# Gated mix of two attentions: where path A's denominators are inverted, and where its late products stand

## The chip, the core and the metric

The kernel runs on one NeuronCore of a Trainium2 chip. The metric is the time of one execution on the device in microseconds; lower is better. The time before is the median of three runs, 987.2 us (984.97 to 989.04).

## What is computed

The input x has 2048 tokens of width 448, in 16 heads of 28. Path A is a linear attention with a learned feature map, path B an ordinary softmax attention, and a gate for each token mixes the two:

```
phi(u) = concat(softmax(u @ w_phi), softmax(-(u @ w_phi)))     per head
kv  = phi(k)^T v;   z = sum over tokens of phi(k)
a   = ((phi(q) kv) / (phi(q) z + 1e-6)) @ woA
b   = softmax(q k^T / sqrt(28)) v @ woB
out = g * a + (1 - g) * b,     g = sigmoid(sum(x * gate_w))
```

The division in path A is by one number per head and token, the **denominator**. All of it is in float32; products that need the precision are split into a high and a low part and run as two or three matmuls.

## The kernel before

The order of the work on PE, DVE, ACT and POOL is the order in which the code is written; only SP's queue of transfers is ordered by a scheduler, from the order of the code and its own estimate of readiness. SP issues its transfers one after another, and each waits in the queue until what it reads is there; what stands behind it waits with it.

The program has three stretches. Up to about 196 us path A's keys, path B's projections and the gate are made. From there to about 332 us runs the stretch that the change is in: path A's queries, numerators, denominators and output, with the first of path B's value projections at its end. From about 364 us on path B's scores and values run (a third of PE's time each), to the end.

The loop of the second stretch counts i; q = i - 16, **y = q - 1**, and tb = y // 2. A path A **block** is 256 tokens, eight blocks (0 to 7) in all; two iterations handle one block. In the order of the code an iteration with q up to 15 projects a tile of queries (`pq`), copies it (`pcq`, ACT), takes its extremes over each head (`extq`, two DVE reductions, L423 and L424), forms the exponents on POOL (L429, L431), and exponentiates them on ACT (L434).

From q = 8 on each iteration has a **unit of maxima** (`mx_unit`, L260 to L265): four small matmuls into four PSUM banks (two `pmd`, two `pmb`), two Relu on ACT (`rl<-pmd`), and two DVE instructions that add and reduce (`rl<-pmb,rl`). These maxima are path B's row maxima. The four banks are the only ones for that use, so a unit's matmuls on PE wait until DVE has read the unit before. Iterations with q from 19 to 25 have a second unit at their end.

The chain of one block b, with the iterations before the change:

- **numerators** (`numer`, L529), at the end of y = 2b + 4: matmuls into two banks `pn`, which ACT copies to `oUa` (L381). Four rows of each bank are the denominators; SP gathers them with two transfers `dena<-oUa` (L384) of 8 KB, spread over 128 partitions.
- **inverses** (`normalize2`), in y = 2b + 5: DVE's RECIPROCAL on `dena` (L389, 128x32), two transfers `rda<-dena` to DRAM (L393), and one transfer `rsa<-rda` (L394) that reads them back repeated over 32 partitions each, 512 KB: the **broadcast**.
- **product** (`normalize3`), in y = 2b + 8: DVE multiplies `oUa` by `rsa` (L400, 128x1024).
- **split** (`normalize4`), in y = 2b + 9: ACT casts `oTa` (L408), POOL subtracts for the low part (L409).
- **output** (`out_a`), in y = 2b + 10 and 2b + 11: twelve matmuls `poa` (L109), which ACT scales by the gate to `ga` (L544); SP stores `gad<-ga` (L545).

`oUa` has three buffers, `dena`, `rda` and `rsa` two each. Iterations with q from 18 on also project a tile of path B's values (`pvb`, eleven matmuls), and transpose features (`pft`, copied by ACT at L519) as long as there are any. SP's queue also carries loads for the maxima (`qp`, `kp`, `kt`, L176).

The part of the loop body that sets the order before the change:

```
if q in (0, 1) or q >= 8:
    mx_unit()
if y >= 9 and y % 2 and tb - 4 < 8:
    oTs[tb - 4] = normalize4(ta, num.pop(tb - 4), f"a{tb - 4}", 2)
...
if y >= 8 and y % 2 == 0 and tb - 4 < 8:
    num[tb - 4] = normalize3(*num[tb - 4], 2)
if y >= 5 and y % 2 and tb - 2 < 8:
    num[tb - 2] = normalize2(ta, *num[tb - 2], f"a{tb - 2}", 2)
```

Of the kernel before, what the change touches and what calls it, by code (L numbers as in the profile page):

```python
# [24 lines left out]
NT = S // P  # L25
# [16 lines left out]
def gated_mix_kernel(ctx, tc, xT, wqkB, wvB, wvA, wkAT, wqAT, phi, woA, woB,  # L42
# [26 lines left out]
    def ps_mx(nm):  # L69
        return ps.tile([P, 512], F32, tag="mx", name=nm, bufs=psn[1])  # L70
# [113 lines left out]
    def mx_load(g, c):  # L184
        mxs[("kc", g, c)] = mx_rows(mx_tile("kc", f"kc{g}_{c}", 5), range(4), k_d[g], range(4),
                                    c * 512)

    def mx_query(gq):
        g, qb = divmod(gq, NQ)
        mxs[("qc", gq)] = mx_rows(mx_tile("qc", f"qc{gq}", 3), range(4), q_d[g], range(4), qb * 512)  # L190

    def pair_load(g, c):

        hp, b = divmod(c, 2)
        heads = (2 * hp, 2 * hp + 1)
        r = mx_tile("kc", f"kp{g}_{c}", 5)
        t = mx_tile("kd", f"kt{g}_{c}", 1)
        mx_rows(r, (0, 1), k_d[g], heads, b * 1024)
        mx_rows(r, (2, 3), k_d[g], heads, b * 1024 + 512)
        mx_rows(t, (2, 3), k_d[g], heads, b * 1024)  # L200
        mxs[("kp", g, c)] = r

        def sub():
            for i in (2, 3):
                js = slice(32 * i, 32 * i + DH)
                nc.gpsimd.tensor_sub(r[js], f32(r[js]), f32(t[js]))

        subs.append(sub)

    def pair_query(gq, hp):  # L210
        g, qb = divmod(gq, NQ)
        mxs[("qp", gq, hp)] = mx_rows(mx_tile("qc", f"qp{gq}_{hp}", 3), range(4), q_d[g],
                                      (2 * hp, 2 * hp + 1) * 2, qb * 512)

    def mx_fin():
        while mxs["fin"]:
            mxs["fin"].pop(0)()
# [5 lines left out]
    def mx_reduce(gq):  # L223

        col = 64 * gq
        n = 2 if gq < GM else 4
        r = 4 * (gq % 8)

        def reduce():
            nc.vector.tensor_reduce(  # L230
                red.rearrange("p (t c) -> p t c", t=4)[:, :, r:r + 4],
                part[:, col:col + 16 * n].rearrange("p (k t h) -> p t h k", t=4, h=4),
                AX.X, ALU.max)
            nm_of[gq] = True

        mxs["fin"].append(reduce)

    def mx_unit():

        u = mxs["u"]  # L240
        if u == NF:
            return
        mx_fin()
        mxs["u"] = u + 1
        gq, r = divmod(u, 16)
        g, qb = divmod(gq, NQ)
        c, qt = divmod(r, 4)
        hp, b = divmod(c, 2)
        col = 64 * gq + 16 * b + 4 * qt + 2 * hp
        if r in (4, 9) and gq + 1 < GM:  # L250
            pair_query(gq + 1, r // 9)
        if r == 4 and gq + 1 == GM:
            mx_query(GM)
        qc, kc = mxs[("qp", gq, hp)], mxs[("kp", g, c)]

        pm = [ps_mx(f"pm{'ddbb'[j]}{u}_{j % 2}") for j in range(4)]
        for j in range(4):
            i = (j + 2) % 4
            js = slice(32 * i, 32 * i + DH)
            nc.tensor.matmul(pm[j], qc[js, qt * P:(qt + 1) * P], kc[js, :], start=True, stop=True,  # L260
                             tile_position=(32 * i, 0))
        for i in range(2):
            rl = rlp.tile([P, 512], F32, tag="rl", name=f"rl{u}_{i}", bufs=psn[2])
            nc.scalar.activation(rl, pm[i], AF.Relu)  # L264
            nc.vector.tensor_tensor_reduce(rl, pm[2 + i], rl, 1.0, LOWEST, ALU.add, ALU.max,  # L265
                                           part[:, col + i:col + i + 1])
        if gq + 1 < GM and qt == 3 and qb == NQ - 1:
            pair_load(g + 1, c)
        if gq + 1 == GM and qt == 3:
            mx_load(GM // NQ, c)  # L270
        if r == 15:
            mx_reduce(gq)
# [114 lines left out]
    def normalize2(pool, oU, den, nm, n):  # L387

        nc.vector.reciprocal(den, den)  # L389
        rd = dr.tile([4, n * 512], F32, tag=f"rd{n}", name=f"rd{nm}", bufs=2)  # L390
        rs = pool.tile([P, n, 512], F32, tag="rs", name=f"rs{nm}", bufs=n)
        for k in range(n):
            nc.sync.dma_start(rd[:, k * 512:(k + 1) * 512], den[:, k, :])  # L393
        nc.sync.dma_start(rs.rearrange("p n q -> p (n q)"),  # L394
                          rd.unsqueeze(1).to_broadcast([4, 32, n * 512]))
        return oU, rs

    def normalize3(oU, rs, n):

        (nc.gpsimd if n == 1 else nc.vector).tensor_mul(oU, oU, rs)  # L400
        return oU

    def normalize4(pool, oU, nm, n):

        oTn = []
        for k in range(n):
            oT = pool.tile([P, 2, 512], F32R, tag="oT", name=f"oT{nm}_{k}", bufs=3 * n - 2)
            (nc.scalar.copy if n == 2 else nc.gpsimd.tensor_copy)(oT[:, 0, :], oU[:, k, :])  # L408
            nc.gpsimd.tensor_sub(oT[:, 1, :], oU[:, k, :], f32(oT[:, 0, :]))  # L409
            oTn.append(oT)  # L410
        return oTn
# [48 lines left out]
    fk, va, fq, fT_of, num, oTs = {}, {}, {}, {}, {}, {}  # L460
# [242 lines left out]
    for i in range(2 * NT + 11):  # L703
        t, q = i, i - NT
        y = q - 1
        tb = y // 2
# [11 lines left out]
        if q == 2:  # L718
            bk_s.close()
            ta_s = ExitStack()  # L720
            ta = ta_s.enter_context(tc.tile_pool(name="ta", bufs=1, reuse_waits="tile"))
# [24 lines left out]
            fk[t - 1] = features2(fk[t - 1], f"k{t - 1}")  # L746
        if q in (0, 1) or q >= 8:
            mx_unit()
        if y >= 9 and y % 2 and tb - 4 < 8:
            oTs[tb - 4] = normalize4(ta, num.pop(tb - 4), f"a{tb - 4}", 2)  # L750
        if q > 0:
# [5 lines left out]
        take_subs()  # L757
        if t == 1:
            pair_load(0, 3)
        if y >= 8 and y % 2 == 0 and tb - 4 < 8:  # L760
            num[tb - 4] = normalize3(*num[tb - 4], 2)
        if y >= 5 and y % 2 and tb - 2 < 8:
            num[tb - 2] = normalize2(ta, *num[tb - 2], f"a{tb - 2}", 2)
        if t < NT:
            value_a(t)
            if t % 2 and t < NT - 4:
# [29 lines left out]
            turn(y - 2)  # L796
        if NT + 3 <= q < NT + 10:
            mx_unit()
        if q == NT + 6:
            ps_s_.close()  # L800
            ps = ps_s_.enter_context(tc.tile_pool(name="psv", bufs=1, space=PSUM, reuse_waits="tile"))
            psn[:2] = 2, 6
# [439 lines left out]
```

## Time and profile before

| | |
|---|---|
| median of three runs | 987.2 us (984.97 to 989.04) |
| the profiled execution's own time | 986.38 us |
| its span, first to last instruction | 984.6 us |
| mean granted TensorE clock | 0.998 |
| PE busy in 196 to 332 us | 131.23 of 136 us |
| DVE busy in 196 to 332 us | 89.08 of 136 us |

The profile is of one execution. The engines are PE (TensorE's matmuls), PEld (its weight loads), DVE (VectorE), ACT (ScalarE), POOL (GpSimd) and SP (SyncE, which issues the transfers; SPq in the rows). A row of a timeline has the start in us from the beginning of the span, the duration in us, the engine, the line of the kernel, the operation, what it writes and reads, the shape, and the number of instructions merged; idle time of the engine before it and what ended that stand in brackets. A row of the chain of waits has start, duration and the piece of work. A row of the stretches has the stretch, its length, busy time of an engine with its number of instructions, the granted clock, the share of the transfer engines in use, and GB/s.

### The profile page before, as it was taken

What the parts mean: (1) busy time and instruction counts of PE and PEld (TensorE: products, weight loads), DVE (VectorE), ACT (ScalarE), POOL (GpSimd) and SP (SyncE); (2) the same over time, 40 slices, a digit from 0 to 9 for tenths busy, and PEclk for the clock granted to TensorE, in tenths of its full rate; (3) what the DMA queues carried; (4) which work ended last, traced back from release to release, by engine and by line L of the source; (5) the groups of instructions that cost most, each with busy time, mean ns of one, the idle gap of its engine ahead of it and who ended that gap; (6) DMA issues with size and microseconds to landing.
All of it is one profiled execution on the core that took longest, in us unless ns stands there. A gap on an engine that the chain in (4) does not pass through costs nothing.

```text
span 984.6 us, 22550 instructions
## 1 busy us (share of the span) xinstructions
PE 973.6 (99%) x8510; PEld 602.9 (61%) x8510; DVE 716.0 (73%) x1338; ACT 752.2 (76%) x1442; POOL 228.1 (23%) x236
## 2 busy tenths in 40 slices
PE   9999999999999999999999999999999999999998
PEld 8777877787767765555555555545555555555555
DVE  5566767888735678888888888888888888885112
ACT  4455655577855688988988888888898898887662
POOL 1135435586732810031011011011011011010010
PEclk9999999999999999999999999999999999999999
DMA  8873110112223234121132121122231222100441
GB/s 295 315 255 114 37 53 32 44 51 73 96 91 100 85 120 130 38 62 41 62 93 69 39 63 41 60 82 66 69 83 41 64 63 65 41 21 30 142 150 57
DMA packets 56140, 84.49 MB, mean 86 GB/s; under 512 B 17216, under 2 KB 23984, under 8 KB 56032
## 3 DMA queue, kind: packets, MB, share of 16 engines
q1 hardware_dynamic: 56032, 83.06, 27.2%
q8 instruction: 67, 1.10, 0.5%
q14 instruction: 41, 0.34, 0.1%
HBM read 54.86 MB, written 27.78 MB: 84 GB/s over the span
## 4 chain that ended last, share of the span: by engine, by line
PE 89%; DMA 6%; DVE 2%; ACT 1%; issue 1%; SPq 0%; DVEq 0%; ACTq 0%
PE g L861 29%; PE pv L1006 26%; PE pk L127 4%; PE pva L127 4%; PE pqk L109 3%; PE g L288 3%; PE pq L109 3%; PE poa L109 3%; PE pob L109 3%; PE pmd L260 3%; DMA dena<-oUa 2%; PE pvb L127 2%; DMA qkd<-ev 2%; PE pvb L109 1%; DMA xraw<-in_xT_dram 1%
## 5 line engine op out<-in xcount | busy, mean ns | idle before, releaser
L869 ACT ACTIVATE p<-g 128x512 f32<-128x512 f32 x1020 | 525.6, 609 | 83.0 <-PE g L861 82.2
L295 DVE TENSOR_REDUCE part<-g 128x1 f32<-128x512 f32 x704 | 442.5, 684 | 83.9 <-PE g L288 82.4
L861 PEld LDWEIGHTS g<-qst,kst 32*128 32x128 f32 x3060 | 221.3, 183 | 215.2 <-DVE part L295 195.0
L861 PE MATMUL g<-qst,kst 32*128 32x512 f32 x3060 | 338.3, 420 | 0.1
L1006 PE MATMUL pv<-p,vb 128*32 128x512 f32 x2048 | 273.0, 605 | 0.0
L288 PE MATMUL g<-kc,qc 28*128 28x512 f32 x704 | 233.5, 495 | 0.0
L265 DVE CUSTOM_DVE_ANT_0 rl<-pmb,rl 128x512 f32<-128x512 f32 x160 | 103.2, 682 | 45.0 <-ACT rl L264 44.9
L400 POOL TENSOR_TENSOR oUb<-oUb,rsb 128x512 f32<-128x512 f32 x15 | 19.3, 1286 | 488.9 <-DMA rsb<-rdb 419.7
L264 ACT ACTIVATE rl<-pmd 128x512 f32<-128x512 f32 x160 | 87.6, 602 | 33.5 <-PE pmb L260 30.1
L288 PEld LDWEIGHTS g<-kc,qc 28*128 28x128 f32 x704 | 86.5, 182 | 0.3
L1006 PEld LDWEIGHTS pv<-p,vb 128*32 128x32 f32 x2048 | 40.6, 108 | 66.1 <-issue 64.2
L109 PE MATMUL pqk<-XH,wB 128*128 128x512 f32 x192 | 59.5, 398 | 0.8 <-DVE ev L569 0.8
L260 PE MATMUL pmb<-kp,qp 28*128 28x512 f32 x160 | 43.1, 498 | 3.3 <-DVE part L265 2.7
L109 PE MATMUL poa<-woA_s,oTa 128*128 128x448 f32 x192 | 45.1, 384 | 0.0
L568 ACT CAST ev<-pqk 128x512 fp32r<-128x512 f32 x28 | 16.0, 588 | 38.0 <-PE pqk L109 21.5
L1017 DVE SCALAR_TENSOR_TENSOR acc<-pob,gate,acc 128x448 f32<-128x448 f32 x12 | 8.2, 684 | 48.4 <-PE pob L109 48.4
L109 PEld LDWEIGHTS pqk<-XH,wB 128*128 128x128 f32 x192 | 35.3, 188 | 9.9 <-issue 1.5
L569 DVE TENSOR_TENSOR ev<-pqk,ev 128x512 fp32r<-128x512 f32 x28 | 18.9, 689 | 29.5 <-ACT ev L568 29.4
L260 PE MATMUL pmd<-kp,qp 28*128 28x512 f32 x160 | 40.1, 497 | 0.0
L109 PEld LDWEIGHTS poa<-woA_s,oTa 128*128 128x128 f32 x192 | 35.7, 193 | 7.0 <-issue 2.5
L127 PE MATMUL pk<-wkA_s,XH 128*128 128x448 f32 x128 | 39.4, 382 | 0.0
L109 PE MATMUL pq<-wqA_s,XH 128*128 128x448 f32 x128 | 37.4, 375 | 1.3 <-ACT oUa L381 1.3
(158 smaller groups left out, 1054.5 us busy)
## 6 DMA issues: line engine op xcount, KB each, us to landing
qkd<-ev SPq DMA_DIRECT2D x28, 512.0 KB
qst<-qkd SPq DMA_DIRECT2D x64, 112.0 KB
kst<-qkd SPq DMA_DIRECT2D x64, 112.0 KB
od<-oTb SPq DMA_DIRECT2D x48, 112.0 KB
rsa<-rda SPq DMA_DIRECT2D x8, 512.0 KB
oL<-od SPq DMA_DIRECT2D x8, 512.0 KB
rsb<-rdb SPq DMA_DIRECT2D x15, 256.0 KB
gad<-ga SPq DMA_DIRECT2D x16, 224.0 KB
```

The lines of the kernel that those rows point to most:

```text
L109: nc.tensor.matmul(dst, l, r, start=i == 0, stop=i == len(todo) - 1)
L127: nc.tensor.matmul(dst[:, :n], l, r, start=i == 0, stop=i == len(todo) - 1, skip_group_check=True)
L260: nc.tensor.matmul(pm[j], qc[js, qt * P:(qt + 1) * P], kc[js, :], start=True, stop=True, tile_position=(32 * i, 0))
L264: nc.scalar.activation(rl, pm[i], AF.Relu)
L265: nc.vector.tensor_tensor_reduce(rl, pm[2 + i], rl, 1.0, LOWEST, ALU.add, ALU.max, part[:, col + i:col + i + 1])
L288: nc.tensor.matmul(pm, mxs[("qc", gq)][js, qt * P:(qt + 1) * P], mxs[("kc", gq // NQ, kb)][js, :], start=True, stop=True, tile_position=(3 ...
L295: nc.vector.tensor_reduce(part[:, col:col + 1], pm, AX.X, ALU.max)
L400: (nc.gpsimd if n == 1 else nc.vector).tensor_mul(oU, oU, rs)
L569: nc.vector.tensor_sub(e[:, 1, :], pq, f32(e[:, 0, :]))
L861: nc.tensor.matmul(st[j], kst_of[(gq // NQ, kt // 4)][js, k, (kt % 4) * P:(kt % 4 + 1) * P], qst_of[gq][js, q, :], start=n == 0, stop=n == ...
L869: nc.scalar.activation(p, st[j], AF.Exp, scale=SCALE)
L1006: nc.tensor.matmul(pv[32 * j:32 * j + 32, :], vb[kt // 8][:, kt % 8, 4 * g + j, :], pt[j], start=kt == 0, stop=kt == NT - 1, tile_position ...
```

## The change

It moves two of a block's steps. The inverses of block b (RECIPROCAL, the two `rda` transfers and the broadcast) are now written in iteration y = 2b + 6, directly behind its first unit of maxima, instead of late in y = 2b + 5. For block 0, whose iteration has no unit, that place is behind the extremes. The products of blocks 4 to 7 (y of 16 and more) are now written at the end of their iteration, behind the numerators, the output and the second unit of maxima where there is one; those of blocks 0 to 3 stay. No instruction is added or removed.

```
         if q in (0, 1) or q >= 8:
             mx_unit()
+        if y >= 6 and y % 2 == 0 and tb - 3 < 8:
+            num[tb - 3] = normalize2(ta, *num[tb - 3], f"a{tb - 3}", 2)
         if y >= 9 and y % 2 and tb - 4 < 8:
...
-        if y >= 8 and y % 2 == 0 and tb - 4 < 8:
+        if y >= 8 and y % 2 == 0 and y < NT and tb - 4 < 8:
             num[tb - 4] = normalize3(*num[tb - 4], 2)
-        if y >= 5 and y % 2 and tb - 2 < 8:
-            num[tb - 2] = normalize2(ta, *num[tb - 2], f"a{tb - 2}", 2)
...
         if NT + 3 <= q < NT + 10:
             mx_unit()
+        if y >= NT and y % 2 == 0 and tb - 4 < 8:
+            num[tb - 4] = normalize3(*num[tb - 4], 2)
```

On PE, ACT and POOL the order stays as it was. It moves on DVE and on SP.

First DVE, from the end of iteration y = 15 on (a name has the block's, tile's or unit's number and then a running number; the read-outs of one number per row behind each rl, the reduction of the maxima and, at the end, unit 50 and what is behind it are left out). Before:

```order
L445 TENSOR_TENSOR fsumq15_3258<-fsumq15_3258,featq15_3160 128x16
L389 RECIPROCAL dena5_3205<-dena5_3205 128x32
L265 ISA rl47_0_3305,part_92<-pmb47_0_3299,rl47_0_3305 128x512
L265 ISA rl47_1_3308,part_92<-pmb47_1_3300,rl47_1_3308 128x512
L400 TENSOR_TENSOR oUa4_3028<-oUa4_3028,rsa4_3111 128x1024
L265 ISA rl48_0_3376,part_92<-pmb48_0_3370,rl48_0_3376 128x512
L265 ISA rl48_1_3379,part_92<-pmb48_1_3371,rl48_1_3379 128x512
L389 RECIPROCAL dena6_3333<-dena6_3333 128x32
L265 ISA rl49_0_3452,part_92<-pmb49_0_3446,rl49_0_3452 128x512
L265 ISA rl49_1_3455,part_92<-pmb49_1_3447,rl49_1_3455 128x512
L400 TENSOR_TENSOR oUa5_3202<-oUa5_3202,rsa5_3265 128x1024
```

and now:

```order
L445 TENSOR_TENSOR fsumq15_3258<-fsumq15_3258,featq15_3154 128x16
L265 ISA rl47_0_3299,part_92<-pmb47_0_3293,rl47_0_3299 128x512
L265 ISA rl47_1_3302,part_92<-pmb47_1_3294,rl47_1_3302 128x512
L389 RECIPROCAL dena5_3205<-dena5_3205 128x32
L400 TENSOR_TENSOR oUa4_3028<-oUa4_3028,rsa4_3173 128x1024
L265 ISA rl48_0_3376,part_92<-pmb48_0_3370,rl48_0_3376 128x512
L265 ISA rl48_1_3379,part_92<-pmb48_1_3371,rl48_1_3379 128x512
L265 ISA rl49_0_3446,part_92<-pmb49_0_3440,rl49_0_3446 128x512
L265 ISA rl49_1_3449,part_92<-pmb49_1_3441,rl49_1_3449 128x512
L389 RECIPROCAL dena6_3332<-dena6_3332 128x32
L400 TENSOR_TENSOR oUa5_3202<-oUa5_3202,rsa5_3307 128x1024
```

Each RECIPROCAL has gone behind one more unit of maxima (47, 49); the product of block 5 has gone behind the second unit of its iteration too (unit 50).

Next SP's queue in the same stretch, from the transfers of block 4's inverses to block 5's broadcast, no row left out. Before:

```order
L393 DMA rda4_3110<-dena4_3031 4x32x16 x2
L394 DMA rsa4_3111<-rda4_3110 128x1x1024
L384 DMA dena5_3205<-oUa5_3202 128x1x16 x2
L545 DMA gad1_70<-ga4_3221 128x448
L545 DMA gad1_70<-ga5_3294 128x448
L393 DMA rda5_3264<-dena5_3205 4x32x16 x2
L176 DMA qp4_0_3578<-qkd_68 28x512 x2
L384 DMA dena6_3333<-oUa6_3330 128x1x16
L394 DMA rsa5_3265<-rda5_3264 128x1x1024
L384 DMA dena6_3333<-oUa6_3330 128x1x16
```

and now:

```order
L393 DMA rda4_3172<-dena4_3031 4x32x16 x2
L384 DMA dena5_3205<-oUa5_3202 128x1x16 x2
L545 DMA gad1_70<-ga4_3221 128x448
L394 DMA rsa4_3173<-rda4_3172 128x1x1024
L545 DMA gad1_70<-ga5_3288 128x448
L176 DMA qp4_0_3572<-qkd_68 28x512 x2
L393 DMA rda5_3306<-dena5_3205 4x32x16 x2
L384 DMA dena6_3332<-oUa6_3329 128x1x16 x2
L176 DMA qp4_0_3572<-qkd_68 28x512
L394 DMA rsa5_3307<-rda5_3306 128x1x1024
```

The gathering of a block's denominators now stands ahead of the broadcast of the block before it (`dena5` ahead of `rsa4`, both halves of `dena6` ahead of `rsa5`), and so it goes on to `dena7` and `rsa6`; the store of `ga4` has come to stand ahead of block 4's broadcast.

Last DVE at the first block, around the end of iteration y = 5, as one piece of the difference:

```order
 L445 TENSOR_TENSOR fsumq5_2498<-fsumq5_2498,featq5_2430 128x16
+L423 TENSOR_REDUCE extq7_2530<-pcq7_2528 128x16
+L424 TENSOR_REDUCE extq7_2530<-pcq7_2528 128x16
 L389 RECIPROCAL dena0_2461<-dena0_2461 128x32
-L423 TENSOR_REDUCE extq7_2536<-pcq7_2534 128x16
-L424 TENSOR_REDUCE extq7_2536<-pcq7_2534 128x16
```

Block 0's RECIPROCAL has gone behind the two extremes of query tile 7; in SP's queue block 0's transfers keep their order among themselves.

## The prediction

> **What bounds the kernel now.** I read the page first, its busy times and the chain of work that ended last:
>
> ```profile
> PE 973.6 (99%) x8510; PEld 602.9 (61%) x8510; DVE 716.0 (73%) x1338; ACT 752.2 (76%) x1442; POOL 228.1 (23%) x236
> PE 89%; DMA 6%; DVE 2%; ACT 1%; issue 1%; SPq 0%; DVEq 0%; ACTq 0%
> ```
>
> PE is busy for 99% of the span. So only what makes PE wait, or run slowly, can be won, and whatever makes it wait anew is lost. Next come the waits of DVE and the pieces of the chain between 260 and 300 us:
>
> ```profile
> DVE dena L389 <- DMA dena<-oUa: 18.7, 6, 7.7
> ```
>
> ```profile
> 263.18 7.40 DMA dena<-oUa
> 274.56 8.31 DMA dena<-oUa
> 284.11 1.95 DMA rda<-dena
> ```
>
> DVE stands for 18.7 us in six waits, the longest 7.7 us, until a block's denominators have been gathered. An 8 KB transfer takes 8 us here, though `rda`, of the same size, takes 1.95. SP's queue shows why:
>
> ```profile
> 273.93 0.54 SPq L394 DMA_DIRECT2D rsa<-rda  x1
> 274.56 0.54 SPq L384 DMA_DIRECT2D dena<-oUa  x1
> ```
>
> The second half of block 6's denominators was issued behind the 512 KB broadcast of block 5 and landed at 274.56 + 8.31 = 282.87. The RECIPROCAL then started at 283.06; block 7's started at 295.09:
>
> ```profile
> 283.06 0.35 DVE L389 RECIPROCAL dena<-dena 128x32 f32<-128x32 f32 x1 [7.67 <-DMA dena<-oUa]
> 295.09 0.35 DVE L389 RECIPROCAL dena<-dena 128x32 f32<-128x32 f32 x1 [5.13 <-DMA dena<-oUa]
> ```
>
> DVE's 18.7 us are not PE's. The timeline of PE tells what reaches it:
>
> ```profile
> 282.93 0.50 PE L260 MATMUL pmd<-kp,qp 28*128 28x512 f32 x2
> 284.03 1.10 PE L260 MATMUL pmb<-kp,qp 28*128 28x512 f32 x2 [0.59 <-DVE part L265]
> 285.06 0.67 PE L109 MATMUL pvb<-wvB_s,XH 128*128 128x448 f32 x2
> ...
> 287.48 0.51 PE L260 MATMUL pmd<-kp,qp 28*128 28x512 f32 x2
> ...
> 287.92 2.71 PE L109 MATMUL poa<-woA_s,oTa 128*128 128x448 f32 x12
> ...
> 293.43 0.49 PE L260 MATMUL pmd<-kp,qp 28*128 28x512 f32 x2
> 296.06 1.11 PE L260 MATMUL pmb<-kp,qp 28*128 28x512 f32 x2 [2.14 <-DVE part L265]
> 297.09 4.05 PE L109 MATMUL poa<-woA_s,oTa 128*128 128x448 f32 x12
> 301.07 0.68 PE L260 MATMUL pmd<-kp,qp 28*128 28x512 f32 x2
> ...
> 301.69 0.67 PE L109 MATMUL pvb<-wvB_s,XH 128*128 128x448 f32 x2
> ```
>
> An undisturbed unit of maxima costs PE 287.92 - 287.48 = 0.44 us, since its four matmuls run side by side. Two units here wait for their banks, held by maxima that queue on DVE behind the waiting RECIPROCAL. The twelve `poa` behind the longer wait are also slow:
>
> ```profile
> 298.00:301.50 3.50, 3.50 (x13) 0.51 0.46 130
> ```
>
> In this stretch PE was granted 0.51 of its clock.
>
> **What goes.** The first unit: 285.06 - 282.93 = 2.13, less 0.44, is 1.69. The second: 297.09 - 293.43 = 3.66, less 0.44, is 3.22. The slow clock: these `poa` took 4.05, those at 287.92 took 2.71, so 1.34; the unit behind them took 301.69 - 301.07 = 0.62, so 0.18 more, together 1.52. With both waits gone 1.69 + 3.22 + 1.52 = **6.43 us** go. They go if `dena` lands before its RECIPROCAL. It is now issued ahead of the broadcast, and the RECIPROCAL stands an iteration later; an iteration (unit, `poa`, unit, `pvb`) takes 293.43 - 287.48 = 5.95. A free gathering should take about what `rda` takes, 1.95; even at 8 us it would be in time, since more than one and a half iterations, 9 us, lie between the numerators at the end of one even iteration and the RECIPROCAL behind the first unit of the next.
>
> A smaller wait goes as well:
>
> ```profile
> 244.96 0.76 PE L260 MATMUL pmb<-kp,qp 28*128 28x512 f32 x2
> 235.93 0.35 DVE L389 RECIPROCAL dena<-dena 128x32 f32<-128x32 f32 x1 [3.10 <-DMA dena<-oUa]
> ```
>
> This `pmb` took 0.76 where an undisturbed one takes 0.51 like its `pmd`: **0.25** too much, with DVE late from its wait of 3.10 for block 2. The other waits of DVE before 275 us lie beside PE that never stops; they are worth nothing.
>
> **What is late next: block 0.** Its RECIPROCAL moves behind two reductions, and everything of its broadcast with it:
>
> ```profile
> 214.05 0.35 DVE L389 RECIPROCAL dena<-dena 128x32 f32<-128x32 f32 x1
> 214.32 0.56 DVE L423 TENSOR_REDUCE extq<-pcq 128x16 f32<-128x448 f32 x1
> 214.79 0.60 DVE L424 TENSOR_REDUCE extq<-pcq 128x16 f32<-128x448 f32 x1
> ...
> 225.77 0.19 DVE L445 TENSOR_TENSOR fsumq<-fsumq,featq 128x16 f32<-128x16 f32 x1
> 226.09 1.22 DVE L400 TENSOR_TENSOR oUa<-oUa,rsa 128x1024 f32<-128x1024 f32 x1
> ```
>
> ```profile
> 217.06 0.53 SPq L394 DMA_DIRECT2D rsa<-rda  x1
> ```
>
> ```profile
> 226.00:226.50 0.50, 0.41 (x1) 1.00 0.05 16
> 226.10:230.00 3.90, 3.90 (x4) 1.00 0.14 44
> ```
>
> The product starts at 226.09, just when the transfers fall silent (0.05 of them busy from 226.0 on). So the broadcast, 226.09 - 217.06 = 9.03 us from its issue, has no slack. The RECIPROCAL would start where the reductions end without it, at 214.05 + 2 x 0.53 = 215.11: 1.06 later. The broadcast waits for `rda`, not for SP, so the product comes **1.05** later. PE feels it at the next unit but one:
>
> ```profile
> 230.04 0.68 DVE L265 CUSTOM_DVE_ANT_0 rl<-pmb,rl 128x512 f32<-128x512 f32 x1
> ```
>
> ```profile
> 230.51 0.51 PE L260 MATMUL pmd<-kp,qp 28*128 28x512 f32 x2
> 230.78 1.11 PE L260 MATMUL pmb<-kp,qp 28*128 28x512 f32 x2
> 231.81 1.09 PE L529 MATMUL pn<-fT,KV 57*32 57x256 f32 x32
> ```
>
> This unit already takes 231.81 - 230.51 = 1.30: its `pmb` start when DVE has read the unit before, at 230.04 and after. From the product to there DVE is busy without a gap (3.90 of 3.90 us), and PE is full from there on; so 1.05 is paid in full. The ends: 0, if the broadcast flies a microsecond faster than now; 1.95, if the three `qp` loads, which are now issued right behind it, cost it the 0.9 by which the two landings behind a broadcast differ, 7.40 and 8.31. I take 1.05, by the rows of this very transfer.
>
> **Block 4's product.** The late products wait for broadcasts that are issued later:
>
> ```profile
> 261.79 1.08 DVE L443 TENSOR_REDUCE featq<-featq 128x32 f32<-128x896 f32 x1
> 274.38 1.18 ACT L408 CAST oTa<-oUa 128x512 fp32r<-128x512 f32 x2
> 275.41 1.19 ACT L519 COPY fT<-pft 128x384 f32<-128x384 f32 x3
> 276.47 0.57 PE L109 MATMUL pvb<-wvB_s,XH 128*128 128x448 f32 x2
> ```
>
> The RECIPROCAL of block 4 goes to where L443 starts behind the maxima of y = 14, 261.79, and by then all is 0.8 later (1.05 - 0.25): 262.6. From RECIPROCAL to broadcast takes 217.06 - 214.05 = 3.0, so 265.6. A broadcast is in after at most 9.03, as above, or 282.87 - 273.93 = 8.94, as block 5's, behind which a gathering had landed by then: 274.5 to 274.6, and the product ends 1.22 later, at 275.8. DVE has nothing else to do before the maxima of y = 17, whose banks PE needs again only an iteration later. But ACT waits with the casts, and behind them stands the copy of `pft` that frees a bank for `pvb`. The casts may start late by 0.66 (276.47 less 275.41 and 0.40 for the first of three copies) at no cost: 274.38 + 0.8 + 0.66 = 275.84. So PE waits just about nothing; with the store of `ga4` ahead of the broadcast, perhaps 0.2 to 0.5; with a landing 1 us later still, 1.2. I take **0.2**.
>
> The products of blocks 5, 6 and 7 move behind a second unit. From a RECIPROCAL behind the first unit to a product behind the second unit two iterations on pass 2 x 5.95 + 0.44 + 2.71 = 15.0 us; from RECIPROCAL to landing 3.0 + 9.03 = 12.0. That leaves 3 us, for block 5 some 2 less, whose `rda` flies behind block 4's broadcast. The casts of these blocks stand on ACT behind the next iteration's first Relu, so a product one unit later hardly moves them. I price them at nothing; what hides them is the 3 us, and the slack of casts and subtractions:
>
> ```profile
> 275.12 2.54 POOL L409 TENSOR_TENSOR oTa<-oUa,oTa 128x512 fp32r<-128x512 f32 x2 [4.93 <-ACT oTa L408]
> ```
>
> From the first cast to the last subtraction pass 275.12 + 2.54 - 274.38 = 3.28 us, and `poa` stands an iteration behind the casts: 5.95 - 3.28 = 2.7 us of slack.
>
> **The sum.** 986.4 (the profiled execution's own time) - 6.43 - 0.25 + 1.05 + 0.2 = 981.0. The median of the runs is 0.8 above the profiled execution, so I put the forecast for it at **981.8 us**, a gain of 5.4.
>
> [...] The stretch at 0.51 stands behind a wait of 2.14 us; the wait of 0.59 at 284.03 has no slow `poa` behind it (2.71). [...]
>
> **Rivals.**
>
> - **The slow clock stays**, or comes at another place: 1.52 is not won, 982.5, or 983.3 for the median. For it: the unit at 230.51 will take 1.30 + 1.05 = 2.35, about as disturbed as the one at 282.93. Against it: that one, 2.13 long, was followed by no slow clock.
> - **Broadcasts are the new wait**: the upper ends, 1.95 and 1.2, and the slow clock: 986.4 - 6.68 + 1.95 + 1.2 + 1.52 = 984.4, or 985.2. For it: block 0 has no slack and block 4 none to spare. Against it: the broadcasts in the rows differ little from one another.
> - **Late products starve the output**, slower than before. Product, casts, subtractions and `poa` are one line with 2.7 us of slack; once the product is later than that, each microsecond costs PE one, in each of blocks 4 to 7. At 5 us late it is 4 x 2.3 = 9.2: 987.2 - 6.7 + 1.25 + 9.2 = 991.0. It decides from 2.7 + 5.4 / 4 = 4.1 us on. For it: all four products now end an iteration, behind maxima that wait for PE. Against it: 3 us are left for the broadcasts, and then 2.7 more.
> - **Nothing changes**: `dena` lands late wherever it is issued, 987.2. Against it: `rda`, as large, lands in 1.95.
>
> **How the numbers follow.** Forecast 0.55, slow clock 0.18, new wait 0.15, starved output 0.08, nothing 0.04. The first three reach from 979.5 (no price for block 0, and a microsecond of spread between runs) to 986.0, and hold over 8 in 10. A measurement of this kernel can tell about 0.5% from no change, 4.9 us: below 982.3 is faster. Of the forecast's 0.55 I put 0.38 below that, of the slow clock's 0.18 0.04: faster 0.42; slower 0.08; the rest, 0.50, within 0.5%.
>
> **What would show it.** Right: no wait of DVE for `dena`; units of 0.44 at the two places, granted clock 1.00 all through 290 to 310; the product of block 0 about 1 us later than 226.09, and the unit of 230.51 about 2.3 us long. Wrong: waits of DVE at L400, in blocks 1 to 3 above all; PE waiting for `oTa` or for copies of `pft` after 275 us; a granted clock below 1 elsewhere in 196 to 332.

## The result and the profile after

The changed kernel takes 979.61 us, the median of six runs (978.86 to 1024.43), beside 987.62 us for the kernel before, measured with it (six runs, 984.97 to 989.25). The recorded ratio is 0.9929, with a 95% interval of 0.9914 to 0.9945 (the two medians alone give 0.9919): a gain of about 0.7%, small, but the interval excludes 1. The run of 1024.43 had a mean granted clock of 0.851 and is left out of the ratio. The profiled execution took 979.64 us, 6.74 less than that of before; its span is 977.9.

The page's busy line and its chain of waits:

```profile
PE 970.2 (99%) x8510; PEld 600.8 (61%) x8510; DVE 715.9 (73%) x1338; ACT 751.8 (77%) x1442; POOL 227.4 (23%) x236
PE 93%; DMA 3%; DVE 2%; issue 1%; ACT 1%; SPq 1%; POOL 0%; DVEq 0%; POOLq 0%; ACTq 0%
```

PE's share of the chain rose from 89% to 93%, that of the transfers fell from 6% to 3%. The timeline of PE at the two places where it waited:

```profile
282.88 0.50 PE L260 MATMUL pmd<-kp,qp 28*128 28x512 f32 x2
282.89 0.50 PE L260 MATMUL pmb<-kp,qp 28*128 28x512 f32 x2
283.32 0.67 PE L109 MATMUL pvb<-wvB_s,XH 128*128 128x448 f32 x2
...
291.68 0.50 PE L260 MATMUL pmd<-kp,qp 28*128 28x512 f32 x2
291.68 0.50 PE L260 MATMUL pmb<-kp,qp 28*128 28x512 f32 x2
292.12 2.71 PE L109 MATMUL poa<-woA_s,oTa 128*128 128x448 f32 x12
294.76 0.50 PE L260 MATMUL pmd<-kp,qp 28*128 28x512 f32 x2
```

Both units take 0.44 us (283.32 - 282.88, 292.12 - 291.68), and the `poa` behind the second take 2.71. The granted clock, in the stretches:

```profile
290.00:310.00 20.00, 19.66 (x106) 1.00 0.48 138
298.00:301.50 3.50, 3.21 (x20) 1.00 0.47 99
```

It is 1.00 in all of 196 to 332. On DVE no instruction waits for `dena` any more; these are the products of blocks 0 and 4, the subtraction behind the first of them, and the inverses of blocks 6 and 7:

```profile
226.51 1.24 DVE L400 TENSOR_TENSOR oUa<-oUa,rsa 128x1024 f32<-128x1024 f32 x1 [0.92 <-DMA qp<-qkd]
227.68 1.08 DVE L144 TENSOR_TENSOR wvB_s<-wvB_raw,wvB_s 128x896 fp32r<-128x896 f32 x1
...
273.52 1.23 DVE L400 TENSOR_TENSOR oUa<-oUa,rsa 128x1024 f32<-128x1024 f32 x1 [3.19 <-DMA rsa<-rda]
281.23 0.35 DVE L389 RECIPROCAL dena<-dena 128x32 f32<-128x32 f32 x1
294.08 0.35 DVE L389 RECIPROCAL dena<-dena 128x32 f32<-128x32 f32 x1
```

The RECIPROCALs at 281.23 and 294.08 have no wait in brackets, where those of before had 7.67 and 5.13. New are the waits ahead of the two products: 0.92 us for block 0 (the row names a load, but the chain below runs through the broadcast) and 3.19 us for block 4's broadcast. PE feels a part of the second: ACT's cast waits for the product, the copy of `pft` stands on ACT behind the cast, and PE waits for the copy:

```profile
274.78 1.14 ACT L408 CAST oTa<-oUa 128x512 fp32r<-128x512 f32 x2 [0.98 <-DVE oUa L400]
276.35 0.67 PE L109 MATMUL pvb<-wvB_s,XH 128*128 128x448 f32 x2 [0.45 <-ACT fT L519]
```

The chain of waits now runs through two broadcasts, of block 0 and of block 4:

```profile
217.48 8.94 DMA rsa<-rda
...
264.40 9.09 DMA rsa<-rda
```

**A measure for what follows.** Executions of one and the same kernel reach the place of the change at different times (the first query projection starts at 181.51 in the profile of before, 180.91 after, 184.00 in e10, with the same code up to there). So the kernels are compared below by one stretch of the profiled execution as well: from the start of the first `pq` to the start of the last unit of maxima. The two ends in the changed kernel:

```profile
180.91 0.47 PE L109 MATMUL pq<-wqA_s,XH 128*128 128x448 f32 x1
...
350.01 0.50 PE L260 MATMUL pmd<-kp,qp 28*128 28x512 f32 x2
```

and before:

```profile
181.51 0.47 PE L109 MATMUL pq<-wqA_s,XH 128*128 128x448 f32 x1
...
356.50 0.50 PE L260 MATMUL pmd<-kp,qp 28*128 28x512 f32 x2
```

The stretch takes 169.10 instead of 174.99 us: 5.89 of the 6.74 come from it. The rest lies where the code did not change: 0.60 ahead of it and 0.25 behind it.

| kernel | median us (runs) | ratio to before, 95% | stretch us |
|---|---|---|---|
| before | 987.62 (6) beside the change; 986.0 (17) beside e1 to e4, 986.52 (12) beside e5 to e8, 985.19 (9) beside e9 to e11 | | 174.99 |
| the change | 979.61 (6) | 0.9929 [0.9914, 0.9945] | 169.10 |
| e1, inverses only | 981.12 (5) | 0.995 [0.9934, 0.9966] | 169.30 |
| e2, products only | 985.87 (12) | 1.0002 [0.999, 1.0014] | 174.67 |
| e3, block 0 back | 979.12 (5) | 0.9926 [0.9911, 0.9941] | 169.50 |
| e4, gathering on ACT's queue | 980.14 (6) | 0.995 [0.9932, 0.9968] | 168.86 |
| e5, block 7's inverses only | 983.11 (7) | 0.9966 [0.995, 0.9982] | 170.69 |
| e6, block 6's inverses only | 979.51 (5) | 0.9926 [0.9914, 0.9939] | 168.67 |
| e7, early splits | 979.19 (4) | 0.9924 [0.991, 0.9938] | 168.57 |
| e8, early splits, block 4 back | 979.65 (5) | 0.9933 [0.9919, 0.9946] | 168.57 |
| e9, first subtraction later | 978.5 (1) | | 168.13 |
| e10, block 4's product back | 982.03 (1) | | 168.35 |
| e11, e9 and e10 | 979.23 (5) | 0.9939 [0.9925, 0.9952] | 168.54 |

### The profile page after: what moved, and what is told of

Same layout as the page of the kernel before. It is cut to its first block, busy times and chain, and to the rows that moved or that the text cites. A ratio compares the mean times of both kernels' runs of the same rounds, so it can differ in the third digit from the quotient of the medians.

```text
span 977.9 us, 22543 instructions
## 1 busy us (share of the span) xinstructions
PE 970.2 (99%) x8510; PEld 600.8 (61%) x8510; DVE 715.9 (73%) x1338; ACT 751.8 (77%) x1442; POOL 227.4 (23%) x236
## 4 chain that ended last, share of the span: by engine, by line
PE 93%; DMA 3%; DVE 2%; issue 1%; ACT 1%; SPq 1%; POOL 0%; DVEq 0%; POOLq 0%; ACTq 0%
PE g L863 29%; PE pv L1008 27%; PE pqk L109 5%; PE pk L127 4%; PE pva L127 4%; PE g L288 3%; PE poa L109 3%; PE pmd L260 3%; PE pob L109 3%; PE pq L109 3%; PE pvb L127 2%; PE pvb L109 2%; DMA rsa<-rda 2%; PE pqk L630 1%; PE pkv L468 1%
```

## The experiments

**Which half of the change wins.** e1 moves the inverses and leaves all products where they were; e2 does the opposite. e1, against before:

```
+        if y >= 6 and y % 2 == 0 and tb - 3 < 8:
+            num[tb - 3] = normalize2(ta, *num[tb - 3], f"a{tb - 3}", 2)
...
-        if y >= 5 and y % 2 and tb - 2 < 8:
-            num[tb - 2] = normalize2(ta, *num[tb - 2], f"a{tb - 2}", 2)
```

> The kernel before with the inverses of all blocks moved as in the change, the late products left in the middle of their iteration. Theory (the waits on the gathered denominators were the whole loss, the place of the late products is worth little): the two waits of PE at 282.93 and 293.43 are gone, span about 978.5. Rival (late products need their new place, since the broadcasts are now issued later): block 5's product stands on DVE ahead of the second unit of maxima of its iteration and waits for a broadcast that in the changed kernel landed near 284.5, just when that unit should be read; PE then loses 0.5 to 1.5 us at the unit near 285.7, and perhaps as much for block 6: span 979 to 980.5.

The inverses alone bring 0.5% and take 5.69 of the 5.89 us out of the stretch. What the late products add shows at block 5. Its product, at the old place, waits for its broadcast ahead of a unit:

```profile
283.42 1.23 DVE L400 TENSOR_TENSOR oUa<-oUa,rsa 128x1024 f32<-128x1024 f32 x1 [2.51 <-DMA rsa<-rda]
```

```profile
285.10 0.50 PE L260 MATMUL pmd<-kp,qp 28*128 28x512 f32 x2
285.31 1.11 PE L260 MATMUL pmb<-kp,qp 28*128 28x512 f32 x2
286.34 2.71 PE L109 MATMUL poa<-woA_s,oTa 128*128 128x448 f32 x12
```

DVE reads the unit before only behind this product, and the unit at 285.10 takes 1.24 us instead of 0.44. So the late products win 0.80 at this unit, and the rival was right for block 5; block 6's units take 0.44, as the theory had it. Over the whole stretch the late products are worth only 0.20 (169.30 against 169.10), since e1 loses nothing at block 4, where the change loses 0.68 (below). e2, against before:

```
-        if y >= 8 and y % 2 == 0 and tb - 4 < 8:
+        if y >= 8 and y % 2 == 0 and y < NT and tb - 4 < 8:
...
+        if y >= NT and y % 2 == 0 and tb - 4 < 8:
+            num[tb - 4] = normalize3(*num[tb - 4], 2)
```

> The kernel before with only the products of blocks 4 to 7 moved to the end of their iteration. Theory (the gain is that of the inverses alone): DVE still waits for the denominators of blocks 5, 6 and 7, PE loses 1.69, 3.22 and the slow clock as before; span 984 to 985, ratio 1.000. Rival (the products in the middle hold up the maxima): a part of the gain, span 981 to 983.

The products alone bring nothing. The waits list of DVE still has

```profile
DVE dena L389 <- DMA dena<-oUa: 17.6, 5, 7.8
```

and PE, behind the second wait, is slow as before:

```profile
294.89 1.10 PE L260 MATMUL pmb<-kp,qp 28*128 28x512 f32 x2 [2.25 <-DVE part L265]
295.92 4.28 PE L109 MATMUL poa<-woA_s,oTa 128*128 128x448 f32 x12
```

**Is it the place in SP's queue?** e4 changes nothing but the queue from which path A's gatherings are issued: ACT's, not SP's, so that they no longer stand behind a broadcast.

```
-            nc.sync.dma_start(den[:, i, :], oU[DH:P:32, i, :])
+            (nc.scalar if n == 2 else nc.sync).dma_start(den[:, i, :], oU[DH:P:32, i, :])
```

> The kernel before, with path A's gatherings of denominators issued from ACT's queue, behind the copies that they read, instead of from SP's; inverses and products where they were. Theory (a gathering is late because it stands behind a 512 KB broadcast in the same queue): it lands in about 2 us whatever flies, all waits of DVE for it go, and so do PE's; block 0's broadcast and block 4's stay early, so the price that the change pays there goes too: span 977.0 to 977.9, at least as good as the change. Rival (the transfer engines are busy with the broadcast whichever queue issues): DVE still waits up to 7 us, span 983 to 985. [...]

Everything else stands in its old place, and yet the wait is nearly gone:

```profile
DVE dena L389 <- DMA dena<-oUa: 1.3, 1, 1.3
```

18.7 us became 1.3, the granted clock is 1.00, and the stretch is 6.13 us shorter. (Its span, 978.3, is 0.4 above what the theory said.) Why the waits went, the issues show. ACT gathers block 6's denominators as soon as it has copied the numerators, and SP sends block 5's broadcast 3 us later (in the kernel before, SP had not come to the second half of that gathering until 274.56):

```profile
270.29 1.16 ACTq L384 DMA_DIRECT2D dena<-oUa  x2
```

```profile
273.47 0.55 SPq L394 DMA_DIRECT2D rsa<-rda  x1
```

The one wait that is left is block 5's, whose gathering was issued right behind block 4's broadcast, in a queue of its own:

```profile
260.98 0.54 SPq L394 DMA_DIRECT2D rsa<-rda  x1
```

```profile
261.56 1.18 ACTq L384 DMA_DIRECT2D dena<-oUa  x2
```

```profile
270.20 0.35 DVE L389 RECIPROCAL dena<-dena 128x32 f32<-128x32 f32 x1 [1.25 <-DMA dena<-oUa]
```

It landed about 8 us after its issue, as if it stood in SP's queue; the theory's 2 us did not hold for it. So it is being issued ahead of the broadcast that helps; a second queue helped here because nothing in it held the gathering back until then. The packets of the trace fit this: the broadcast's 128 packets of 4 KB run from 262.32 to 268.59, and of the gathering's 256 packets of 64 bytes the first starts at 265.69, only 67 start before the broadcast's last packet has ended, and the last ends at 269.54. Why most of the gathering, in a queue of its own, still came behind the broadcast, the trace does not show.

**One block at a time.** e5 and e6 move the inverses of a single block, 7 or 6. e6, against before (e5 has y == 20 and 7):

```
+        if y == 18:
+            num[6] = normalize2(ta, *num[6], "a6", 2)
...
-        if y >= 5 and y % 2 and tb - 2 < 8:
+        if y >= 5 and y % 2 and tb - 2 < 8 and tb - 2 != 6:
```

> Before, with only block 7's inverses moved behind the first unit of the next iteration. Theory (the RECIPROCAL's wait for the gathering holds up the unit behind it; the slow clock follows the long wait): the wait of PE at the unit near 293 goes, 3.22 us, and with it the slow stretch behind it, 1.52; the smaller wait near 283 stays at about 2.1 us for its unit. Span about 984.6 - 4.7 = 979.9, granted clock 1.00 all through 290 to 310. Rival (the slow clock has a cause of its own): only 3.2 goes, span about 981.4, and a stretch below 1.00 of some 3.5 us stands somewhere between 285 and 310.

In the profiled execution the second wait and the slow clock go together, as the theory had it; the clock is 1.00 in 290 to 310. The first wait stayed, and was longer in this execution:

```profile
281.90 0.50 PE L260 MATMUL pmd<-kp,qp 28*128 28x512 f32 x2
283.90 1.11 PE L260 MATMUL pmb<-kp,qp 28*128 28x512 f32 x2 [1.50 <-DVE part L265]
284.94 0.68 PE L109 MATMUL pvb<-wvB_s,XH 128*128 128x448 f32 x2
```

Its unit loses 284.94 - 281.90 - 0.44 = 2.60 us, where the same code lost 1.69 before: PE came to it 1.03 earlier (281.90, not 282.93), while the RECIPROCAL started almost when it did before (282.94, not 283.06). So the stretch is 4.30 shorter rather than 4.74, and the span 979.5. The median of the runs, 983.11, is 1.8 above the profiled execution. The runs' mean granted clocks say why in part: 1.000 in four (980.97 to 983.11), 0.997 or 0.998 in the three longest (983.68 to 985.12). In those a slow clock was left; where, is not on record.

The length of PE's wait alone does not set the slow clock. Behind the wait of 1.50 above there was none, but e10 (below) has one far ahead of the change, in code that is the same in all these kernels, behind this wait:

```profile
60.54 1.11 PE L260 MATMUL pmb<-kp,qp 28*128 28x512 f32 x2 [0.79 <-DVE part L265]
```

Its unit took 61.58 - 59.26 = 2.32 us, and from 61.70 to 65.11 the granted clock was 0.50: three pairs `pqk<-XH` took 1.14, 1.05 and 1.03 us there, the next one, at 65.33, 0.63. The stretch is 3.41 us long, like those of before (298.07 to 301.48) and e2 (295.95 to 299.36). This is most of why e10 comes to its first `pq` 3.1 us later than the change. In the 3.41 us ahead of the slow stretch PE was busy for 2.50 us in e10, 1.90 before and 1.04 in e2; in e5 it was busy for 1.78 of the 3.40 us from 282.40 on, and no slow stretch followed. So this busy time does not tell the cases apart either, and the condition stays open.

> Before, with only block 6's inverses moved. Theory: the unit near 283 falls from 2.13 to 0.44 us, 1.69 goes, while the unit near 292 still waits over 2 us and the stretch behind it is still granted about 0.51; span about 982.9. Rival (the wait only moves on: the second unit waits longer by what the first one lost): the second unit grows from 3.66 to about 5 us and the span stays within 0.5 us of 984.6.

Neither theory nor rival foresaw this: one block's inverses, moved alone, bring as much as the whole change (0.9926 and 0.9929). The waits of DVE for `dena` are still 9.7 us in sum, but block 7's RECIPROCAL, which was **not** moved, has none:

```profile
287.34 0.35 DVE L389 RECIPROCAL dena<-dena 128x32 f32<-128x32 f32 x1
```

The reason stands in SP's queue. Before:

```profile
283.45 1.22 SPq L393 DMA_DIRECT2D rda<-dena  x2
...
286.12 0.54 SPq L394 DMA_DIRECT2D rsa<-rda  x1
286.71 1.18 SPq L384 DMA_DIRECT2D dena<-oUa  x2
```

and in e6:

```profile
283.17 1.15 SPq L393 DMA_DIRECT2D rda<-dena  x2
284.40 1.16 SPq L384 DMA_DIRECT2D dena<-oUa  x2
285.74 0.53 SPq L394 DMA_DIRECT2D rsa<-rda  x1
```

Block 6's broadcast is now issued behind block 7's gathering. Whether block b's gathering lands late is thus decided by where the inverses of block b - 1 stand. In e6 block 6's own RECIPROCAL still waited (2.31 us), but behind its unit, at the price of 0.53 us at the unit of 284.94. The change has two remedies for each wait: the gathering goes ahead of the broadcast (e6, for block 7), and the RECIPROCAL comes an iteration later (e5, for block 7). Either of them alone is enough for block 7.

**Block 0.** e3 is the change with block 0's inverses alone back at their old place:

```
+        if y >= 8 and y % 2 == 0 and tb - 3 < 8:
...
+        if y == 5:
+            num[0] = normalize2(ta, *num[0], "a0", 2)
```

> The changed kernel with block 0's inverses back at their old place, all else as changed. Theory of the plain sum: the product of block 0 comes 1.05 us earlier and PE's unit of maxima near 230 gets shorter by as much as it grew, 1.56 back to 1.30, and no more, since its growth was only 0.26; span about 977.6. The 0.26, where 1.05 was forecast, I put down to the subtraction of a weight on DVE behind the product: 1.83 us before and 1.08 in the changed kernel, because POOL's multiplication of the features ran while DVE waited for the broadcast instead of beside it. If so, here that subtraction takes 1.83 us again and POOL's multiplication about 2.0. Rival (the 0.75 is chance of that run): the subtraction takes 1.1 us here too, and the unit comes 0.75 earlier than in the kernel before; span about 976.9.

```profile
225.69 1.23 DVE L400 TENSOR_TENSOR oUa<-oUa,rsa 128x1024 f32<-128x1024 f32 x1
226.83 1.83 DVE L144 TENSOR_TENSOR wvB_s<-wvB_raw,wvB_s 128x896 fp32r<-128x896 f32 x1
```

```profile
229.96 0.50 PE L260 MATMUL pmd<-kp,qp 28*128 28x512 f32 x2
230.38 1.11 PE L260 MATMUL pmb<-kp,qp 28*128 28x512 f32 x2
231.42 0.88 PE L529 MATMUL pn<-fT,KV 57*32 57x256 f32 x24
```

The product starts 0.82 earlier than in the change (225.69, not 226.51), but L144 takes 1.83 instead of 1.08, and the unit 1.46 instead of 1.56: by this pair block 0's later inverses cost PE 0.10 us. That is less than the spread: the unit takes 1.18 to 1.82 us in the six kernels with block 0's inverses at the old place (before and e2 to e6), and 1.43 to 1.56 in the three where only their place is new there (the change, e1, e10). (e3's stretch is longer than the change's, 169.50, by what it loses at block 4, below.) Where the 0.75 of L144 went, POOL's rows say. In e3, and then in the change:

```profile
225.71 2.01 POOL L446 TENSOR_TENSOR featq<-featq,fsumq 128x448 f32<-128x448 f32 x1 [1.53 <-DVE fsumq L445]
```

```profile
225.73 0.94 POOL L446 TENSOR_TENSOR featq<-featq,fsumq 128x448 f32<-128x448 f32 x1 [1.53 <-DVE fsumq L445]
```

With the early product, L446 starts 0.02 behind it and takes 2.01 us (0.94 with the late one), and L144, beside it up to 225.71 + 2.01 = 227.72, takes 1.83 (1.08 with the late one). With the late product, L446 is done (225.73 + 0.94 = 226.67) not long after the product has begun, while DVE waits for the broadcast. The time between is booked as busy time. It is not chance of one run: in before, e2 to e6 and e10, where L446 starts behind the product, it takes 1.79 to 2.01 and L144 1.83; in the change and e1, where it starts ahead of it, they take 0.94 and 1.08. What holds the two instructions up, the rows do not show.

**What is left at the unit of 230.** Three more kernels try to win the remaining 1.12 us (1.56 - 0.44) there, and the 0.68 at block 4. e7 is the change with both splits of path B's value weights an iteration earlier:

```
-        if q in (8, 10):
-            split_part(wvB_s, "wvB", D, (q - 8) // 2)
+        if q in (7, 9):
+            split_part(wvB_s, "wvB", D, (q - 7) // 2)
```

> The changed kernel, with the two splits of path B's value weights written one iteration earlier, so that their subtractions (L144) no longer stand on DVE behind the products of blocks 0 and 1. It asks what is left of the wait of PE at the unit near 230, which took 1.56 us in the changed kernel, 1.12 above an undisturbed one. Theory (DVE's backlog of product and subtraction holds the unit's banks): without the subtraction of 1.08 us behind the product the unit takes 0.44 to 0.7 us, the span is about 0.9 below that of the changed kernel, near 977.0; the moved subtraction is hidden in DVE's idle 0.19 and 0.92 us ahead of the product. Rival (the product alone, which waits for the broadcast, holds the unit): the unit stays above 1.2 us and the span at 977.9.

The unit falls to 0.43 (231.10 to 231.53), so DVE's backlog of product and subtraction is what held it. But the cast (L143), which moved along, now stands on ACT ahead of the copies of block 0's numerators:

```profile
214.99 0.67 PE L109 MATMUL pq<-wqA_s,XH 128*128 128x448 f32 x2 [1.39 <-ACT oUa L381]
```

That wait was 0.55 in the change. Of the 1.12 won, 0.84 is lost there, and the second cast costs another 0.50 (PE's wait for the copies of block 1 is 1.32, not 0.82). The stretch is 0.53 shorter than the change's all the same, but that much lies at block 4 alone (a loss of 0.15 instead of 0.68, below), not at the splits. e9 leaves the cast and moves only the first subtraction:

```
-        take_lows()
+        if q != 9:
+            take_lows()
```

> The changed kernel, with the first subtraction for path B's value weights (L144) left standing until the next iteration, behind a unit of maxima, while its cast on ACT stays in place. In the kernel with both splits written earlier the unit near 230 fell to 0.43 us, but the cast, moved with them, let PE wait 1.39 instead of 0.55 for the numerators' copies before 217. Theory (the subtraction behind block 0's product is what the unit waits for; the cast is what cost PE time in the other kernel): the unit near 230 takes 0.44 us, PE's wait before 217 stays near 0.55, and the stretch from the first query projection to the last unit of maxima falls from 169.10 to about 168.0. Rival (the subtraction behind the next unit stands in the way there): PE's next unit, near 238, or its copies of pft lose what the one at 230 wins, and the stretch stays at 169.

```profile
229.81 0.50 PE L260 MATMUL pmd<-kp,qp 28*128 28x512 f32 x2
229.82 0.62 PE L260 MATMUL pmb<-kp,qp 28*128 28x512 f32 x2
231.01 1.15 PE L529 MATMUL pn<-fT,KV 57*32 57x256 f32 x32 [0.57 <-ACT fT L519]
```

The unit is free, yet PE stops 0.57 us behind it for copies that stand on ACT behind the cast of the second split (L143, at 229.55). From unit to numerators pass 1.20 us, against 1.56 in the change. ACT was the second bound, 0.36 us below DVE. The stretch, 168.13, is near the 168.0 that was expected, but not for the reason given: 0.36 of the 0.97 was won here, and 0.46 at block 4 (below).

**Block 4.** e8 is e7 with block 4's inverses back at y = 13; e10 is the change with block 4's product at its old place; e11 is e10 and e9 in one kernel.

```
-        if y >= 6 and y % 2 == 0 and tb - 3 < 8:
+        if y >= 6 and y % 2 == 0 and tb - 3 < 8 and tb - 3 != 4:
...
+        if y == 13:
+            num[4] = normalize2(ta, *num[4], "a4", 2)
```

> As the kernel with the early splits, and block 4's inverses put back to where they stood before the change. Theory (block 4's product waits for its later broadcast and delays ACT's casts, behind which PE's wait for the copy of pft stands): the product of block 4 ends about 1.4 us earlier than in the changed kernel, PE's wait of 0.45 for the copy of pft goes, and the unit behind it comes 0.6 us earlier; the gathering of block 5 lands late again, but its RECIPROCAL waits under 1 us, which PE does not feel. Span about 0.6 below that of the kernel with the early splits alone, near 976.4. Rival (the copies of pft are late by themselves, or the wait moves to block 5): PE still waits about 0.5 us between 270 and 290, and the span does not move.

```
-        if y >= 8 and y % 2 == 0 and y < NT and tb - 4 < 8:
+        if y >= 8 and y % 2 == 0 and y <= NT and tb - 4 < 8:
...
-        if y >= NT and y % 2 == 0 and tb - 4 < 8:
+        if y > NT and y % 2 == 0 and tb - 4 < 8:
```

> The changed kernel, with block 4's product alone put back to its old place ahead of the numerators (those of blocks 5 to 7 stay late; the inverses stay where the change put them). On DVE this changes no order unless a unit or a reduction stood between the two places. Theory (block 4's product waits for the broadcast, wherever it is written, and the casts behind it): PE still waits about 0.45 us for the copy of pft near 276 and the stretch from the first query projection to the last unit stays at 169.1, within 0.2. Rival (the late place itself delays the casts): that wait goes, and the stretch falls by 0.6.

> Both edits together: the first subtraction for path B's value weights left until the next iteration, and block 4's product at its old place. Theory: the sum of what the two do alone; if only the first helps, the stretch from the first query projection to the last unit takes about 168.0 us and the execution about 978.4; if both help, 167.4 and 977.8. Rival: no less than the changed kernel's 169.1.

By the expectations, e8 should have won 0.6 on e7 and won nothing, and e10 should have won nothing and won 0.75 in its stretch, with no wait of PE at block 4; e11, with the same place of the product, had that wait again (0.40) and was 0.19 longer than e10 in all. So it is not the place of the product. One number orders the kernels whose product of block 4 waits for its broadcast: how long after the start of the unit in y = 17 it starts. In the change that is 273.52 - 271.92 = 1.60. "Loss" is the time from this unit to the next one, less the 6.17 that it takes before (272.66 to 278.83):

| kernel | product behind the unit | unit to unit | loss |
|---|---|---|---|
| e10 | 275.55 - 274.85 = 0.70 | 6.18 | 0.01 |
| e1 | 272.70 - 271.93 = 0.77 | 6.17 | 0.00 |
| e7 | 272.81 - 271.74 = 1.07 | 6.32 | 0.15 |
| e9 | 272.40 - 271.28 = 1.12 | 6.39 | 0.22 |
| e11 | 272.81 - 271.27 = 1.54 | 6.79 | 0.62 |
| the change | 273.52 - 271.92 = 1.60 | 6.85 | 0.68 |
| e3 | 273.85 - 271.81 = 2.04 | 7.31 | 1.14 |

About 0.9 us are free, and beyond that each microsecond costs PE one. In every row the product waits for its broadcast, as in e10:

```profile
275.55 1.22 DVE L400 TENSOR_TENSOR oUa<-oUa,rsa 128x1024 f32<-128x1024 f32 x1 [2.29 <-DMA rsa<-rda]
```

The term of block 4 is thus set by when the broadcast lands, and that swings by 1.3 us against PE (0.70 to 2.04). This is from execution to execution: e1 and the change issued the broadcast at the same time (264.40) and came to the unit at the same time (271.93, 271.92), and the product could start at 272.70 in one and at 273.52 in the other; e10's PE came to this unit 2.93 us later than the change's, its product only 2.03. e8, where the broadcast was issued earlier, has no loss (6.17), but e7 had only 0.15 left to win.

None of these versions can be told from the change by its median: e3, e6, e7, e8 and e11 lie at 979.1 to 979.7, and the single runs of e9 and e10 at 978.5 and 982.0.

## Why the prediction was right, and where its terms were off

The forecast of 981.8 us was 2.2 above the 979.61 measured, which lies in the range, just above its lower end. Direction and mechanism were right; two terms of the sum were mis-sized. Of the 2.2, about 0.5 are terms of the sum (below). The rest the forecast did not foresee: about 0.85 lies outside the stretch, where nothing was changed, and 0.8 was added for the median, which after the change is no higher (979.61) than the profiled execution (979.64). By the two profiled executions:

| step | forecast | measured |
|---|---|---|
| unit at 282.93 | -1.69 | -1.69 (2.13 to 0.44) |
| unit at 293.43 | -3.22 | -3.22 (3.66 to 0.44) |
| slow clock behind it | -1.52 | -1.52 (`poa` 4.05 to 2.71, and the unit behind) |
| unit at 244.96 | -0.25 | -0.25 (0.69 to 0.44) |
| block 0 | +1.05 | +0.26 (unit 1.30 to 1.56) |
| block 4 | +0.2 | +0.68 (6.17 to 6.85) |
| `poa` behind the unit of 244.96 | none | -0.17 |
| sum over the stretch | -5.43 | -5.91 |

- **The waits and the clock** came as forecast, to the hundredth, since what goes can be read off the rows of before. That this slow stretch belonged to the long wait is borne out by four kernels: with a wait of PE of 2.14 or 2.25 there (before, e2) it stands behind it, and with the wait gone (e5, the change) so is the slow clock. The runs fit too: the five of the change that the ratio uses have a mean granted clock of 0.999 or 1.000, and of the 38 of before beside the experiments all but one have 0.995 to 0.998. What sets it in is open: e10 shows one behind a wait of 0.79.
- **The unit at 244.96** came as forecast by luck. In e2, e5 and e6 block 2's inverses stand where they did and DVE waits 2.25 to 2.47 us for them, and yet this unit takes 0.44 and the next one comes 7.22 us behind it, as in the change (7.65 before). So the 0.25 and the 0.17 of the `poa` were of the one execution that was profiled before.
- **Block 0** is the step that failed, in size. "From the product to there DVE is busy without a gap (3.90 of 3.90 us), and PE is full from there on; so 1.05 is paid in full." The product did come 1.01 later, measured from the unit of y = 7 (226.51 - 216.77, less 226.09 - 217.36), as forecast. But DVE's busy 3.90 held 0.75 us by which L144 took longer where POOL's L446 ran beside the product and it (2.01 us), and with the later product L446 (0.94) runs while DVE waits anyway. e3 and the change show both: early product, 1.83; late product, 1.08. The 0.26 in the table also holds run-to-run spread (1.18 to 1.82 at the old place); e3 puts the price of block 0's place at 0.10.
- **Block 4** is the second term that was mis-sized, 0.2 for 0.68. The rows of the prediction were the right ones. It let the product start up to 275.84 - 1.22 - 273.46 = 1.16 us behind the unit (at 272.66 + 0.8 = 273.46); the table gives about 0.92. And it had the product end at 275.8, a start 1.1 behind the unit; it was 1.60. The broadcast itself took 9.09, as long as forecast (9.03), and was issued at 264.40, 1.2 earlier than the 265.6 forecast; but PE, which lost less at block 0 and had started earlier, came to the unit at 271.92, 1.54 earlier. Since the landing swings by 0.8 from execution to execution, one trace can hardly give this term closer than that.
- **The rivals**: the slow clock did not come back in the stretch. Broadcasts are the new wait for blocks 0 and 4, at 0.26 and 0.68, below the rival's 1.95 and 1.2. The late products do not starve the output; e1 shows them to be worth 0.80 at block 5. One of the signs named for being wrong did come: PE waits for a copy of `pft` at 276.35. One named for being right did not: the unit near 230 takes 1.56, not 2.3.
- **The reason given for block 7** was half of it. The prediction had the gathering ahead of the broadcast and the RECIPROCAL an iteration later as one remedy; e5 and e6 show that each does it alone for block 7, and e6 that moving one block's inverses would have been enough.

Between the 981.0 of the sum and the 979.64 of the profiled execution lie 1.36 us: 0.48 are the terms above, and about 0.85 is what lies outside the stretch.

## What to carry to other kernels

When a small transfer takes four times what one of its size takes elsewhere (here 8.31 us and 1.95, both of 8 KB), look at what was issued ahead of it: with the large one issued behind the small one, the wait for the small one went here (5.13 us for block 7 before, none in e6), and one such exchange was enough. Another queue helped here only where it issued the small one earlier (the gathering that it issued behind a broadcast was still awaited for 1.25 us, e4). An engine that shows no gap may still have slack: an elementwise instruction took 1.83 us in one place and 1.08 in another. A term read off one trace of before should be looked for in a second: the wait of PE at 244.96 was in one execution alone. A wait for a transfer should be priced against the engine that will come earlier, not against the times of the old trace.

## What the runs showed of the hardware

- Where POOL's 128x448 product (L446) started just behind DVE's product (before, e3), it took 2.01 us and DVE's 128x896 subtraction (L144) behind that product 1.83; where it started ahead (the change), they took 0.94 and 1.08. The time between is booked as busy time.
- An 8 KB gathering issued behind a 512 KB broadcast took 8.31 us to land in the same queue (274.56 to 282.87, before); in a queue of its own it was issued at 261.56 and awaited until 270.20 (e4). `rda`, of 8 KB too, took 1.95 (before).
- Waits of PE of 2.14 (before), 2.25 (e2) and 0.79 us (e10) were followed by a stretch of 3.41 us at a granted clock of 0.50 (298.07 to 301.48, 295.95 to 299.36, 61.70 to 65.11); one of 1.50 (e5) was not. In these runs the length of the wait alone does not decide.
